# Reordering TensorE's program in a hedgehog-attention plus SwiGLU kernel: filler matmuls, moved query projections, merged evictions, spread gate/up groups

## Chip, cores, metric

One core of one Trainium2 chip. The metric is the device time of one execution in microseconds (us). Profiles show a "span" some 2 us shorter than that time (277.9 where the execution took 279.78). Ratios in this text are the mean time of one kernel's fast runs over the mean of the other's fast runs of the same rounds, so not quite the ratio of the medians quoted beside them.

## The reference, cut to what matters

```python
xn = layernorm(x)                                # x: (1, 2048, 640)
# A: linear attention, 32 heads of 20
q, k, v = split(xn @ wqkv)
phi(t)  = concat(softmax(t @ w_phi), softmax(-(t @ w_phi)))   # 40 features per head
kv = sum_s phi(k) v ; z = sum_s phi(k)
o  = phi(q) @ kv / (phi(q) @ z + 1e-6)
A  = o @ wo
# B: SwiGLU, 640 -> 1536 -> 640
B  = (silu(xn @ w1) * (xn @ w3)) @ w2
out = x + A + B
```

## The kernel before

All work is described as operations with an engine, a modelled duration and dependencies; a small planner puts them in an order per engine. In the profile of this kernel, TensorE (PE) ran nothing else during the 1.40 us that the KV product at 135.53 us waited for phi_k. The names used below, for 16 tiles of 128 tokens in 4 chunks `c` of 512:

- `T(t)`, `V(t)`, `K(t)`: transpose of a tile, value and key projections. `KV(t)`: ten small matmuls that add a tile's phi(k) and v into two PSUM tiles `kva` and `kvb`. `kv_evac`: their masked copy to SBUF (`kvr`).
- `Q(c, g)`: query projection of a chunk, group `g` of 5 (five 128x512 matmuls), followed on ScalarE (ACT) by two exponentials `eq`.
- `RT(t)`: twelve matmuls `eq x kvr`, whose results ACT copies to `rt`; half go to PSUM tiles named `rtbank`, of which there are only two.
- `ATT(pair)`, `OT(pair)`: division on VectorE (DVE), then a store (`od`) and a transposing DMA (`oT`).
- `GU(c, fi)`: one gate/up group, ten 128x512 matmuls, then ACT (`th`, `up`), DVE (`gs`), GpSimd (POOL, `hT`).
- `O(t)`: an output tile, two halves of twelve `w2` and five `wo` matmuls.
- `fill(us)`: puts in as many GU groups as the PE time that is owed.

```python
    def warm():                       # ten 128x512 matmuls at the start
    ...
    def fill(us):
        nonlocal gi, owed
        owed += us
        while owed > 1.1 and gi < limit:
            GU(*gus[gi], modes(gi)); gi += 1
            owed -= 2.16
    ...                               # (cut: the loop over K, V, KV; at its end gi has met limit)
    KV(NST - 2)
    fill(2.2)
    KV(NST - 1)
    kv_evac()                         # 20 evictions of 84 columns
    wo_dma = ...
    for g in range(NQ):
        Q(0, g)

    def attend(pair, us):
        RT(2 * pair); fill(us); RT(2 * pair + 1); ATT(pair); OT(pair); fill(us)

    residual(0)
    limit = 3 * KF
    attend(0, 2.2)
    attend(1, 2.2)
    for i in range(NST // 2):
        nxt = i + 2
        if i % 2 == 0 and nxt // 2 < NSC:
            residual(nxt // 2)
            for g in range(NQ):
                Q(nxt // 2, g)
        if nxt < NST // 2:
            attend(nxt, 2.2)
        if i == 5:
            fill(100)
        O(2 * i)
        O(2 * i + 1)
        if i == 1:
            limit = len(gus)
```

The softmax here doesn't subtract the row's maximum and nothing guards it: scores larger than these inputs give would overflow.

## Time and profile before

| | before |
|---|---|
| time, 4 runs known at the time of the prediction | 285.73 us (285.39 to 285.8) |
| time, 16 runs by the end of the comparison | 285.91 us (285.25 to 288.1) |
| span of the profiled run | 283.3 us |
| PE busy | 271.2 us, 96% |
| last matmul group of PE starts | 278.91 us |

PE is nearly always busy, so what can be won is its holes. The prediction below shows the lines and how a hole is measured from them.

### The profile page before, as it was taken

How to read it: one execution, taken by the hardware profiler on the slowest of the kernel's cores; microseconds unless marked ns; L12 is line 12 of the kernel's file. 1: busy time of each engine (PE TensorE's matmuls, PEld its weight loads, DVE VectorE, ACT ScalarE, POOL GpSimd, SP SyncE). 2: the span in 40 equal slices, each digit the busy share in tenths (PEclk: the TensorE clock that was granted, in tenths of full speed). 3: DMA queues.
4: the chain of work that ended last, by engine and by line, in shares of the span. 5: the costliest groups of instructions: out<-in, count | busy, mean ns of one | idle time of the engine just before them, and what ended most of it. 6: DMA issues, size and time to landing. Idle time of an engine off the chain costs nothing.

```text
span 283.3 us, 4874 instructions
## 1 busy us (share of the span) xinstructions
PE 271.2 (96%) x1863; PEld 163.6 (58%) x1886; DVE 172.0 (61%) x295; ACT 146.1 (52%) x320; POOL 94.6 (33%) x124
## 2 busy tenths in 40 slices
PE   7899999999998999998899999999999999999994
PEld 2545555556565556565445567644457675777773
DVE  4783699979767655668626986414458280657221
ACT  2668766666675767665769904284460508340000
POOL 8734657747546555554032000003331100000000
PEclk9999999999999999999999999999999999999999
DMA  8999995027000700003000344340001316042301
GB/s 220 312 299 249 282 288 189 0 74 175 33 0 0 187 1 2 0 0 119 0 0 2 91 139 98 108 126 0 0 2 44 98 57 175 2 139 70 94 23 46
DMA packets 44614, 26.54 MB, mean 94 GB/s; under 512 B 26288, under 2 KB 44592, under 8 KB 44592
## 3 DMA queue, kind: packets, MB, share of 16 engines
q1 hardware_dynamic: 43936, 26.22, 33.3%
q8 instruction: 14, 0.23, 0.3%
q10 hardware_dynamic: 656, 0.03, 0.2%
q14 instruction: 8, 0.07, 0.1%
HBM read 12.81 MB, written 7.21 MB: 71 GB/s over the span
## 4 chain that ended last, share of the span: by engine, by line
PE 76%; issue 7%; DVE 6%; ACT 5%; DMA 3%; POOL 1%; SPq 1%; DVEq 0%; ACTq 0%; POOLq 0%
PE bank L548 35%; PE bank L790 14%; PE bank L399 12%; PE bank L794 6%; PE bank L636 4%; ACT eq L651 2%; DMA xg<-in_A_x_dram 2%; ACT rt L690 1%; DVE ks L447 1%; PE rtbank L682 1%; PE bank L505 1%; DVE om L731 1%; ACT ek L438 1%; DMA oT<-od 1%; DVE phik L464 1%
## 5 line engine op out<-in xcount | busy, mean ns | idle before, releaser
L548 PE MATMUL bank<-xnT,w 128*128 128x512 bf16 x461 | 108.3, 379 | 1.8 <-DVE gs L569 0.8
L591 POOL TENSOR_TENSOR hT<-gs,up 128x512 bf16<-128x512 bf16 x44 | 50.8, 1155 | 118.5 <-ACT up L586 81.2
L548 PEld LDWEIGHTS <-w 128*128 128x128 bf16 x480 | 46.7, 98 | 51.7 <-issue 1.0
L790 PE MATMUL bank<-w,hT 128*128 128x320 bf16 x384 | 59.1, 299 | 0.0
L569 DVE SCALAR_TENSOR_TENSOR gs<-th,bank 128x512 bf16<-128x512 bf16 x48 | 32.4, 677 | 36.2 <-ACT th L564 36.2
L790 PEld LDWEIGHTS <-hT 128*128 128x128 bf16 x384 | 37.2, 98 | 13.8
L564 ACT ACTIVATE th<-bank 128x512 bf16<-128x512 f32 x48 | 28.9, 602 | 23.0 <-PE bank L548 22.7
L399 PEld LDWEIGHTS <-xnT 128*128 128x128 bf16 x320 | 30.3, 98 | 14.9 <-DVE xnT L385 1.1
L586 ACT ACTIVATE up<-bank 128x512 bf16<-128x512 f32 x44 | 26.3, 597 | 23.4 <-PE bank L548 23.4
L447 DVE TENSOR_REDUCE ks<-ek 128x64 f32<-128x1280 bf16 x16 | 23.6, 1476 | 16.6 <-ACT ek L438 16.5
L651 ACT ACTIVATE eq<-bank 128x512 bf16<-128x512 f32 x40 | 21.4, 649 | 21.6 <-PE bank L636 21.6
L464 POOL TENSOR_TENSOR phik<-ek,kr 128x640 bf16<-128x640 bf16 x16 | 29.1, 1820 | 6.7 <-PE bank L399 3.0
L799 DVE TENSOR_TENSOR res<-bank,xr 128x320 bf16<-128x320 f32 x32 | 15.4, 484 | 23.0 <-PE bank L794 23.0
L794 PE MATMUL bank<-wo,oT 128*128 128x320 bf16 x160 | 26.9, 299 | 0.6 <-DMA oT<-od 0.6
L690 ACT CAST rt<-bank 128x352 bf16<-128x352 f32 x32 | 13.9, 522 | 24.5 <-issue 15.1
L399 PE MATMUL bank<-wv,xnT 128*128 128x320 bf16 x160 | 24.4, 299 | 1.6 <-DVE xnT L385 0.8
L438 ACT ACTIVATE ek<-bank 128x320 bf16<-128x320 f32 x64 | 23.1, 439 | 3.7 <-PE bank L399 3.5
L399 PE MATMUL bank<-wkphi,xnT 128*128 128x320 bf16 x160 | 24.3, 299 | 0.0
L464 DVE TENSOR_TENSOR phik<-ek,kr 128x640 bf16<-128x640 bf16 x16 | 22.1, 1381 | 1.8 <-DVE kr L456 0.5
L636 PE MATMUL bank<-xnT,wqphi 128*128 128x512 bf16 x96 | 22.5, 379 | 0.2
L794 PEld LDWEIGHTS <-oT 128*128 128x128 bf16 x160 | 15.6, 98 | 7.0 <-DMA oT<-od 1.0
L682 PEld LDWEIGHTS <-eq 128*128 128x128 bf16 x192 | 12.8, 98 | 7.1 <-ACT eq L651 2.3
(62 smaller groups left out, 216.4 us busy)
## 6 DMA issues: line engine op xcount, KB each, us to landing
w<-in_B_w_dram SPq DMA_DIRECT2D x8, 480.0 KB, 7.0
xr<-in_A_x_dram SPq DMA_DIRECT2D x4, 640.0 KB, 4.7
od<-om SPq DMA_DIRECT2D x8, 320.0 KB, 2.3
out_dram<-res SPq DMA_DIRECT2D x16, 160.0 KB, 2.0
xg<-in_A_x_dram SPq DMA_DIRECT2D x12, 160.0 KB, 3.8
xnd<-xn SPq DMA_DIRECT2D x3, 640.0 KB, 3.2
w<-in_B_w_dram SPq DMA_DIRECT2D x1, 1920.0 KB, 10.0
wv<-in_A_wqkv_dram SPq DMA_DIRECT2D x2, 400.0 KB, 4.2
```

Of the source, the lines that this page charges most:

```text
L399: nc.tensor.matmul(o["ps"][:], xnT[:, c, t * P : (t + 1) * P], w[:, c, 320 * half : 320 * half + 320], start=(c == 0), stop=(c == KD - 1),)
L447: nc.vector.reduce_sum(out=box["s"][:].rearrange("p a h -> p (a h)"), in_=box["ek"][:].rearrange("p a (h d) -> p (a h) d", d=Dh), axis=AX.X,)
L464: phik_ins[t] = eng.tensor_mul(out=phik_b[t][:, :, sgn, :], in0=box["ek"][:, sgn, :].rearrange("p (h d) -> p h d", d=Dh), in1=box["r"][:, ...
L548: nc.tensor.matmul(o["ps"][:], w[:, k, fi * P : (fi + 1) * P], xs[:, k, :], start=(k == 0), stop=(k == KD - 1))
L564: nc.scalar.activation(out=box["th"][:], in_=og["ps"][:], func=AF.Tanh, scale=0.5)
L569: nc.vector.scalar_tensor_tensor(out=box["gs"][:], in0=box["th"][:], scalar=1.0, in1=og["ps"][:], op0=ALU.add, op1=ALU.mult)
L586: nc.scalar.activation(out=box["up"][:], in_=ou["ps"][:], func=AF.Copy, scale=0.5)
L591: lambda: nc.gpsimd.tensor_mul(out=hT[c][:, fi, :], in0=box["gs"][:], in1=box["up"][:]),
L636: nc.tensor.matmul(o["ps"][:], wqphi[:, k, g * P : (g + 1) * P], xnT[:, k, c * 512 : (c + 1) * 512], start=(k == 0), stop=(k == KD - 1),)
L651: nc.scalar.activation(out=eqt[c, sgn][:, g, 0:512], in_=o["ps"][:], func=AF.Exp, scale=1.0 - 2.0 * sgn)
L790: nc.tensor.matmul(o["ps"][:], hT[c][:, fi, ti * P : (ti + 1) * P], w2[:, fi, cols], start=(fi == 0), stop=False)
L794: nc.tensor.matmul(o["ps"][:], oT[c][:, k, ti * P : (ti + 1) * P], wo_of[0][:, k, cols], start=False, stop=(k == KD - 1))
```

## The change

The intent is to close PE's holes: keep it busy at the start, place the query projections where PE waits for the last keys, evict in fewer instructions, stop gate/up groups from coming in bursts, keep RT groups apart, and do both `w2` halves of the first output tile before its `oT` is needed. Core of the diff:

```diff
+        load_x(xg[1], 0, 4, 1)
         load_gu(0)
-        load_x(xg[1], 0, 4, 1)
...
+    def idle(n):                       # n matmuls 128x256 on a tile of zeros
...
     T(0, "DVE")
+    keep_busy(9)                       # nine of them as one operation of the planner
...
     T(1, "ACT")
+    keep_busy(6)
...
-                    for k in range(g, e):
-                        nc.vector.tensor_mul(out=dst[:, k, ...], in0=v[:, k, ...], in1=m[:, k, ...])
+                    nc.vector.tensor_mul(out=dst[:, g:e, ...], in0=v[:, g:e, ...], in1=m[:, g:e, ...])
...                                     # O(t) is split in first (w2) and second (wo):
+            [(first, 0), (first, 1), (second, 0), (second, 1)] if t == 0
+            else [(first, 0), (second, 0), (first, 1), (second, 1)]
...                                     # in fill():
+        if gi == limit:
+            owed = 0.0
...
+    fill(2.2)
+    Q(0, 0)
     KV(NST - 2)
-    fill(2.2)
+    for g in range(1, 4):
+        Q(0, g)
     KV(NST - 1)
     kv_evac()
     wo_dma = ...
-    for g in range(NQ):
-        Q(0, g)
+    Q(0, 4)
+    fill(2.2); RT(0)                   # RT 1 to 3 likewise, each behind a fill
...                                     # the loop, for i, with nxt = i + 2:
+            fill(2.2); RT(2 * nxt); fill(2.2)
         O(2 * i)
+            RT(2 * nxt + 1); ATT(nxt); OT(nxt)
+        if nxt % 2 == 1 and nxt // 2 + 1 < NSC:
+            for g in range(NQ): Q(nxt // 2 + 1, g)
         O(2 * i + 1)
```

More of the change, by code (lines that the diff above doesn't have):

```diff
@@ L183 @@
     ident = consts.tile([P, P], bf, name="ident")
+    zero = consts.tile([P, 256], bf, name="zero")
     eps = consts.tile([P, 1], f32, name="eps")
@@ L210, in warm, with fn @@
             nc.tensor.matmul(ps[:], xnT[:, 0, 0:P], xnT[:, 0, 0:512])
+    def idle(n):
+        def fn():
+            ps = bank([P, 256], f32)
+            for i in range(n):
+                nc.tensor.matmul(ps[:], zero[:, 0:P], zero[:])
+        return fn
     WARM = 10
@@ L215, in constants @@
         make_identity(nc, ident[:])
+        nc.gpsimd.memset(zero[:], 0.0)
         nc.gpsimd.memset(eps[:], EPS)
@@ L368, in bank, with keep_busy @@
         return ringp.tile(shape, dt, name="bank", tag="bank")
+    def keep_busy(n):
+        u = plan.op("PE", pe_us(n, 256), idle(n), takes="bank")
+        u["frees"].append(u)
+        u["open"] += 1
     def T(t, evac):
@@ L610, in fn @@
                 def fn(g=g, e=e):
-                    for k in range(g, e):
-                        nc.vector.tensor_mul(
-                            out=dst[:, k, offs[g] : offs[g] + 4, 0 : HC - 1],
-                            in0=v[:, k, :, :],
-                            in1=m[:, k, :, None].to_broadcast([64, 4, HC - 1]),
-                        )
-                kvr_of.append(plan.op("DVE", 0.2 * (e - g), fn, deps=[KV_of[NST - 1]]))
+                    nc.vector.tensor_mul(
+                        out=dst[:, g:e, offs[g] : offs[g] + 4, 0 : HC - 1],
+                        in0=v[:, g:e, :, :],
+                        in1=m[:, g:e, :, None].to_broadcast([64, e - g, 4, HC - 1]),
+                    )
+                kvr_of.append(plan.op("DVE", dve_us(84 * (e - g)), fn, deps=[KV_of[NST - 1]]))
                 g = e
@@ L772, in OT, with O @@
         )
-    def O(t):
+    def O(t, between=None):
         c, ti = divmod(t, 4)
@@ L782, in O, with first, fn @@
         rb = plan.alloc("half", al)
-        for half in range(2):
-            cols = slice(320 * half, 320 * half + 320)
-            o = {}
-            def fn(o=o, cols=cols):
+        hs = [dict(cols=slice(320 * h, 320 * h + 320), half=h) for h in range(2)]
+        def first(o):
+            def fn():
                 o["ps"] = bank([P, 320], f32)
@@ L790, in fn, with second, ev @@
                     nc.tensor.matmul(
-                        o["ps"][:], hT[c][:, fi, ti * P : (ti + 1) * P], w2[:, fi, cols], start=(fi == 0), stop=False
+                        o["ps"][:], hT[c][:, fi, ti * P : (ti + 1) * P], w2[:, fi, o["cols"]], start=(fi == 0), stop=False
                     )
+            o["u"] = plan.op("PE", pe_us(KF, 320), fn, deps=GU_of[c], takes="bank", frees=[hT_a[c]])
+        def second(o):
+            def fn():
                 for k in range(KD):
-                    nc.tensor.matmul(o["ps"][:], oT[c][:, k, ti * P : (ti + 1) * P], wo_of[0][:, k, cols], start=False, stop=(k == KD - 1))
-            u = plan.op("PE", pe_us(KF + KD, 320), fn, deps=GU_of[c] + [dep, wo_dma], takes="bank", frees=[oT_a[c], hT_a[c]])
-            def ev(o=o, cols=cols, half=half):
-                nc.vector.tensor_tensor(out=box["res"][:, cols], in0=o["ps"][:], in1=xr[c][:, ti, cols], op=ALU.add)
-                if half == 1:
-                    nc.sync.dma_start(out=out2[t * P : (t + 1) * P, :], in_=box["res"][:])
-            plan.op("DVE", dve_us(320), ev, deps=[u, xr_of[c], rb], frees=[u, xr_a[c]] + [rb] * half)
+                    nc.tensor.matmul(o["ps"][:], oT[c][:, k, ti * P : (ti + 1) * P], wo_of[0][:, k, o["cols"]], start=False, stop=(k == KD - 1))
+            o["v"] = plan.op("PE", pe_us(KD, 320), fn, deps=[o["u"], dep, wo_dma], frees=[oT_a[c]])
+            def ev():
+                nc.vector.tensor_tensor(out=box["res"][:, o["cols"]], in0=o["ps"][:], in1=xr[c][:, ti, o["cols"]], op=ALU.add)
+                if o["half"] == 1:
+                    nc.sync.dma_start(out=out2[t * P : (t + 1) * P, :], in_=box["res"][:])
+            plan.op("DVE", dve_us(320), ev, deps=[o["v"], xr_of[c], rb], frees=[o["u"], xr_a[c]] + [rb] * o["half"])
+        for step in (
+            [(first, 0), (first, 1), (second, 0), (second, 1)] if t == 0
+            else [(first, 0), (second, 0), (first, 1), (second, 1)]
+        ):
+            step[0](hs[step[1]])
     xr_of = {}
@@ L890 @@
     wo_dma = plan.op("SP", 0.5, load_wo, deps=[KV_of[NST - 1]], lat=3.5)
-    for g in range(NQ):
-        Q(0, g)
-    def attend(pair, us):
-        RT(2 * pair)
-        fill(us)
-        RT(2 * pair + 1)
-        ATT(pair)
-        OT(pair)
-        fill(us)
+    Q(0, 4)
     residual(0)
     limit = 3 * KF
-    attend(0, 2.2)
-    attend(1, 2.2)
+    fill(2.2)
+    RT(0)
+    fill(2.2)
+    RT(1)
+    ATT(0)
+    OT(0)
+    fill(2.2)
+    RT(2)
+    fill(2.2)
+    RT(3)
+    ATT(1)
+    OT(1)
+    for g in range(NQ):
+        Q(1, g)
     for i in range(NST // 2):
         nxt = i + 2
-        if i % 2 == 0 and nxt // 2 < NSC:
-            residual(nxt // 2)
-            for g in range(NQ):
-                Q(nxt // 2, g)
         if nxt < NST // 2:
-            attend(nxt, 2.2)
+            if nxt % 2 == 0:
+                residual(nxt // 2)
+            fill(2.2)
+            RT(2 * nxt)
+            fill(2.2)
         if i == 5:
@@ L916 @@
         O(2 * i)
+        if nxt < NST // 2:
+            RT(2 * nxt + 1)
+            ATT(nxt)
+            OT(nxt)
+        if nxt % 2 == 1 and nxt // 2 + 1 < NSC:
+            for g in range(NQ):
+                Q(nxt // 2 + 1, g)
         O(2 * i + 1)
```

## The prediction

> **What bounds the kernel now.** I read the page first (busy shares), then busy time by stretch, then the list of waits, then TensorE's (PE's) timeline around the waits found, and last the order of instructions of both programs on each engine.
>
> ```profile
> PE 271.2 (96%) x1863; PEld 163.6 (58%) x1886; DVE 172.0 (61%) x295; ACT 146.1 (52%) x320; POOL 94.6 (33%) x124
> ```
>
> PE is busy 96% of 283.3 us. Busy includes the modelled tail of each matmul, so short gaps hide in it. The stretches show where idle time lies (columns: stretch, length, busy time of PE, weight loads, DVE, ACT, POOL, each with a count):
>
> ```profile
> 5.00:15.00 10.00, 7.87 (x62) 5.14 (x61) 7.93 (x25) 5.85 (x13) 7.58 (x36) 1.00 1.14 311
> 126.00:136.00 10.00, 8.29 (x85) 5.82 (x85) 6.55 (x6) 5.65 (x15) 4.32 (x3) 1.00 0.26 84
> 150.00:164.00 14.00, 12.85 (x105) 7.77 (x105) 11.82 (x24) 12.50 (x31) 1.15 (x1) 1.00 0.22 60
> 190.00:235.00 45.00, 44.74 (x282) 26.45 (x286) 25.09 (x42) 15.85 (x32) 9.22 (x8) 1.00 0.11 34
> 255.00:283.30 28.30, 24.75 (x183) 17.61 (x180) 9.27 (x17) 0.00 (x0) 0.00 (x0) 1.00 0.19 58
> ```
>
> The reader is to see that 190 to 235 us runs without gaps, so this program can feed PE, and that holes stand at the start, at 126 to 136, at 150 to 164, and at the very end (the last eviction and store). The waits of PE itself (total, times, longest):
>
> ```profile
> PE kva L481 <- DVE phik L464: 1.4, 1, 1.4
> PE bank L794 <- DMA oT<-od: 0.6, 1, 0.6
> PE rtbank L682 <- ACT rt L690: 0.5, 3, 0.2
> PE kva L481 <- POOL phik L464: 0.3, 1, 0.3
> PE bank L682 <- ACT eq L651: 0.2, 1, 0.2
> ```
>
> and the places on PE's timeline (start, length, line, operation, count, wait):
>
> ```profile
> 131.48 0.20 PE L481 MATMUL kva<-vaug,phik 128*128 128x84 bf16 x1
> ...
> 135.53 0.20 PE L481 MATMUL kva<-vaug,phik 128*128 128x84 bf16 x1 [1.40 <-DVE phik L464]
> ...
> 140.01 0.44 PE L682 MATMUL bank<-kvr,eq 128*128 128x154 bf16 x5
> ...
> 149.63 0.51 PE L682 MATMUL bank<-kvr,eq 128*128 128x154 bf16 x6
> ...
> 157.68 0.37 PE L682 MATMUL bank<-kvr,eq 128*128 128x154 bf16 x4
> ...
> 163.73 0.85 PE L794 MATMUL bank<-wo,oT 128*128 128x320 bf16 x5 [0.64 <-DMA oT<-od]
> ```
>
> The 1.40 us is the last KV product (line 481) waiting for the last phi_k; 163.73 is the first output tile waiting for its transposed attention output.
>
> [...] a group of ten 128x512 matmuls advances 2.16 us. [...] here the wait at 135.53 held up everything behind it. So what counts is the order on PE. [...] here the ten warm-up matmuls take 4.45 us (half rate) and the first projection at 7.05 runs at full rate; the largest wait of PE before 15 us is 1.24. [...] Below, 20 evictions of 84 elements take about 177 ns each [...].
>
> **Method.** I count PE's time in issue steps read from this timeline, not in busy time: 0.216 us per 128x512 matmul, 0.136 per 128x320 (17 in 2.31), 0.0573 in RT (24 in 1.375), 0.0385 in KV (10 in 0.385). Stretch minus work is time lost:
> - 131.86 (131.48 + 10 KV) to 140.01: 20 KV 0.77 + 25 Q matmuls 5.40 = 6.17 of 8.15; lost 1.98.
> - to 149.63: one RT 0.69 + 40 gate/up (GU) matmuls 8.64 = 9.33 of 9.62; lost 0.29.
> - to 157.68: three RT 2.06 + Q 5.40 = 7.46 of 8.05; lost 0.59 (three RT in a row wait for ACT to empty the two extra PSUM banks).
> - to 163.73: two RT 1.38 + 24 w2 matmuls 3.26 = 4.63 of 6.05; lost 1.42 (exponentials of Q, then the oT transfer).
> - to PE's last issue, about 279.6: 520 output matmuls 70.6 + ten RT 6.9 + two Q 10.8 + twelve GU 25.9 = 114.2 of 115.9; lost 1.65, at 170 to 172, 182 to 188, 239 to 243 and 250 to 253, where RT follows RT or Q.
>
> In all 1.98 + 0.29 + 0.59 + 1.42 + 1.65 = 5.93 us. That is all that a perfect order after 131.86 could win.
>
> **The change part by part.** The programs' orders on PE differ only by the two fillers until 131.86.
>
> *Start.* Nine zero matmuls after transpose 0 and six after transpose 1, 128x256: about 0.107 each at full rate, 0.96 and 0.64 us. The holes there are 0.83 to 1.1 and 0.79 us, so they fit; at half rate nine take 1.9 and push projection 0 from 7.05 to about 8.0. Its end, 9.3 instead of 8.4, then passes transpose 1's start at 9.11: cost 0 to 0.3. No gain, since the clock is already at full rate. Moving the second x block (640 KB) ahead of the first gate/up weights (2 x 480 KB) keeps the same bytes ahead of both: x lands near 10.3 instead of 12.5 and the weights near 12.5, estimated from x landing 7.7 us after issue at 4.84 and 300 GB/s. The weights are first used at 15.04 and DVE turns to that x only after 12.9. Worth 0.
>
> *KV end.* Q groups 0 to 3 now stand around KV 14 and 15. KV 15 comes 131.86 + 1.08 + 0.39 + 3.24 = 136.57, after phi_k (135.5); KV 14 at 132.94, after its own (132.3). Both waits vanish.
>
> *kvr.* Twenty DVE evictions, 3.55 us, become eight of the same elements. [...]
>
> ```profile
> 136.07 0.85 DVE L612 TENSOR_TENSOR kvr<-kva,mask 64x84 bf16<-64x84 f32 x5 [0.69 <-PE kvb L481]
> ```
>
> They begin at about 137.1 and end at 139.6. Ahead of RT 0 PE has Q group 4 and one GU: 136.96 + 1.08 + 2.16 = 140.2. The merge is needed for this order but by itself off the path.
>
> *Spreading.* Setting owed to zero removes the bursts of four and ten GUs; one GU goes between RTs. Per step PE needs 2.85 us; ACT two evictions at 0.6 and four rt copies at 0.343 (twelve in 4.11), 2.57. ACT keeps up, the PSUM waits go. Q 1 then RT 4 remains adjacent: ten exponentials take 5.17 to 5.4 us against PE's 5.4, so the last ends about 1.2 to 1.4 us after Q while RT's other ten matmuls and three of w2 fill 1.0. I keep a loss of 0.4. Q 2 and Q 3 now have a whole output tile behind them.
>
> *First output.* Both w2 halves go first. Attention of pair 0 ends on DVE near 152.0 (rt copies done 145.3, then 5.3 us of its own work and two gs); plus 2.3 for od and 3.7 for oT gives 158.0. PE arrives after RT 1 to 4, three more GUs, Q 1 and 24 w2 matmuls, at about 159.3. No wait. At the other end, RT 15 ends near 251, its oT lands near 265, and tile 14 needs it after 266: no wait, 1.7 us to spare.
>
> **Sum.** 5.93 won; 0.4 left at RT 4; 0.4 kept for small new waits and the fillers: 5.1 us. 285.73 - 5.1 = 280.6.
>
> **Rivals.**
> 1. *Perfect packing*: PE loses nothing after 131.86: 285.73 - 5.93 = 279.8. For: 190 to 235 us is nearly free of gaps. Against: ACT is busy 12.50 of 14 us in 150 to 164, and it is still behind Q 1.
> 2. *A new wait replaces the old*: DVE or ACT, in order, are held by an attention step or a th whose source is late, and the spread GUs feel it each time. For: each GU needs ACT, then DVE, and DVE now has gs inside attention. Twelve to sixteen places at 0.15 would give back 2: 282.5.
> 3. *The start gets worse*: fillers at half rate, or weights late. Loses 0.3 to 1; with the main gain 281 to 281.6.
> 4. *Holes were hidden anyway*: that would need another bound, but PE is the last engine throughout; the idle DVE and ACT time after 163 speaks against it. Then 285.
>
> **Range and chances.** Faster by over 2% means below 280.0, a gain of 5.7 out of 5.93: nearly perfect packing. I give it 0.22. Between 280.0 and 282.5, small remains or rival 2, is the bulk; slower by 2% would need a stall of 10 us, 0.01. Range 279.4 to 282.5.
>
> **What would show it.** Right: no wait of a kva/kvb matmul on phi_k; no wait of the first wo matmul on oT; eight kvr evictions of about 2.5 us in all; RT waits on rt copies gone; RT 4's first matmul near 155 and the first wo matmul near 159 us; fillers ahead of the first projections, with GU still starting near 15.0. Wrong: PE idle by DVE's gs or ACT's th between 140 and 260, a wait on w1 near 15 us, a later first projection, or a wait for oT at tile 14.

## The result and the profile after

| | before | after |
|---|---|---|
| median time | 285.91 us (285.25 to 288.1, 16 runs) | 279.84 us (279.5 to 280.43, 11 runs) |
| ratio | | 0.9782, 95% interval 0.9761 to 0.9803 |
| span of the profiled run | 283.3 | 277.9 |
| start of PE's last matmul group | 278.91 | 273.35 |
| start of the first `wo` group | 163.73 | 159.11 |

The kernel is 2.2% faster; the interval straddles the 2% line, so whether the gain passes 2% is unclear. Busy time of the changed kernel in stretches like those of the prediction (length, then PE, weight loads, DVE, ACT, POOL, then granted clock, DMA share and GB/s):

```profile
5.00:15.00 10.00, 9.59 (x77) 6.66 (x76) 7.89 (x26) 5.78 (x13) 7.83 (x37) 1.00 1.16 288
126.00:136.00 10.00, 9.95 (x86) 6.55 (x86) 6.56 (x6) 7.06 (x18) 4.31 (x3) 1.00 0.27 84
150.00:164.00 14.00, 14.00 (x103) 8.76 (x101) 11.04 (x20) 9.06 (x21) 1.61 (x1) 1.00 0.37 92
190.00:235.00 45.00, 44.79 (x326) 29.22 (x329) 24.39 (x44) 17.81 (x40) 3.46 (x3) 1.00 0.22 64
```

PE went from 8.29 to 9.95 of 10 us in the second stretch and from 12.85 to 14.00 of 14 in the third, while ACT fell there from 12.50 to 9.06. In the first stretch the new busy time is the fillers, which compute nothing. All waits of PE that remain in the changed kernel (total, times, longest):

```profile
PE bank L211 <- DVE xnT L208: 1.2, 1, 1.2
PE bank L563 <- DVE gs L584: 0.8, 1, 0.8
PE bank L392 <- DVE xn L337: 0.3, 1, 0.3
```

The waits on phi_k, oT, rt copies and eq are gone from this list. The three that it has are not new: the kernel before has the same kinds (xnT 1.2, gs 0.8, xn 0.5), and two further waits for xnT of 0.8 each. The prediction's list, which shows five of the ten, left them out. PE's timeline of the changed kernel, at the places that answer to those of before (L496 is the KV product, L696 RT, L803 `w2`, L812 `wo`):

```profile
136.59 0.20 PE L496 MATMUL kva<-vaug,phik 128*128 128x84 bf16 x1
...
140.21 0.51 PE L696 MATMUL bank<-kvr,eq 128*128 128x154 bf16 x6
...
154.84 0.44 PE L696 MATMUL bank<-kvr,eq 128*128 128x154 bf16 x5
...
155.69 0.24 PE L696 MATMUL bank<-kvr,eq 128*128 128x154 bf16 x1
...
156.18 0.24 PE L696 MATMUL rtbank<-kvr,eq 128*128 128x154 bf16 x1
...
159.11 1.52 PE L812 MATMUL bank<-wo,oT 128*128 128x320 bf16 x10
...
273.35 0.84 PE L812 MATMUL bank<-wo,oT 128*128 128x320 bf16 x5
```

The last KV product stands at 136.59 without a wait (predicted 136.57), RT 0 at 140.21 (140.2), RT 4 at 154.84 ("near 155"), the first `wo` matmul at 159.11 ("about 159.3"). From the end of KV 13 to PE's last issue (last group's start plus 5 x 0.136) before took 279.59 - 131.86 = 147.73 us and after 274.03 - 131.90 = 142.13, for work of 141.8: of 5.93 us lost there, 5.6 are won and 0.3 remain, most of it around the two single matmuls at 155.69 and 156.18, gaps of some 0.15 us each, too short for the list of waits; ACT ends the last exponentials of Q 1 near 156.1.

### The profile page after: what moved, and what is told of

It is laid out like the page before. It is cut to its first block, busy times and chain, and to the rows that moved or that the text cites. A ratio compares the mean times of both kernels' runs of the same rounds, so it can differ in the third digit from the quotient of the medians.

```text
span 277.9 us, 4892 instructions
## 1 busy us (share of the span) xinstructions
PE 270.5 (97%) x1877; PEld 165.6 (60%) x1901; DVE 173.1 (62%) x283; ACT 146.5 (53%) x320; POOL 95.4 (34%) x125
## 4 chain that ended last, share of the span: by engine, by line
PE 91%; DVE 2%; DMA 2%; issue 1%; POOL 1%; ACT 1%; SPq 1%; POOLq 0%
PE bank L563 35%; PE bank L803 19%; PE bank L414 14%; PE bank L812 8%; PE bank L650 8%; PE bank L696 2%; PE rtbank L696 2%; DMA xg<-in_A_x_dram 2%; PE bank L520 1%; PE kva L496 1%; PE kvb L496 1%; POOL phik L479 1%; DVE gs L584 0%; ACT ek L453 0%; POOL rstd L308 0%
## 5 line engine op out<-in xcount | busy, mean ns | idle before, releaser
L606 POOL TENSOR_TENSOR hT<-gs,up 128x512 bf16<-128x512 bf16 x44 | 51.2, 1165 | 140.2 <-ACT up L601 91.7
L803 PE MATMUL bank<-w,hT 128*128 128x320 bf16 x384 | 57.5, 299 | 0.0
L803 PEld LDWEIGHTS <-hT 128*128 128x128 bf16 x384 | 37.4, 98 | 15.0
L704 ACT CAST rt<-bank 128x352 bf16<-128x352 f32 x32 | 12.9, 458 | 29.7 <-PE bank L696 25.9
L812 PE MATMUL bank<-wo,oT 128*128 128x320 bf16 x160 | 26.8, 299 | 0.0
L812 PEld LDWEIGHTS <-oT 128*128 128x128 bf16 x160 | 15.7, 98 | 6.1
L650 PEld LDWEIGHTS <-wqphi 128*128 128x128 bf16 x100 | 9.5, 98 | 10.4
```

Source lines behind the costliest of these rows:

```text
L606: lambda: nc.gpsimd.tensor_mul(out=hT[c][:, fi, :], in0=box["gs"][:], in1=box["up"][:]),
L650: nc.tensor.matmul(o["ps"][:], wqphi[:, k, g * P : (g + 1) * P], xnT[:, k, c * 512 : (c + 1) * 512], start=(k == 0), stop=(k == KD - 1),)
L803: nc.tensor.matmul(o["ps"][:], hT[c][:, fi, ti * P : (ti + 1) * P], w2[:, fi, o["cols"]], start=(fi == 0), stop=False)
L812: nc.tensor.matmul(o["ps"][:], oT[c][:, k, ti * P : (ti + 1) * P], wo_of[0][:, k, o["cols"]], start=False, stop=(k == KD - 1))
```

## The experiments

Twelve runs were made, one of them the changed kernel again, each with a correct result and timed in rounds against the kernel before on the same chip. "Part undone" kernels are the changed kernel less one part; "part alone" kernels are the kernel before plus one. The differences in us below are between medians, 279.84 for the changed kernel and, for parts alone, the median of before of the same rounds. The parts undone ran in other rounds than those that gave 279.84; the changed kernel, repeated beside c_all, gave 279.81.

### Parts undone

**Fillers out (a_nofill).** Edit:

```diff
-    keep_busy(9)
-    keep_busy(6)
```

> The changed kernel without its fifteen zero matmuls at the start. Theory (the prediction's): [...] they are worth 0 in a typical execution: 279.8 +- 0.3, gate/up starting at 15.0 to 15.1 us. Rival: they keep the PE clock up; then projections 0 and 1 run at half rate without them in the profile, or some executions come out 1.5 to 2.5 us above the rest, as three of the sixteen executions of the kernel before did (287.6 to 288.1), while none of eleven of the changed kernel did.

Measured 280.68 us median (279.87 to 283.77, 6 runs), ratio to before 0.9829 (interval 0.9777 to 0.9882). Two of six executions were at 282.85 and 283.77, the fastest at 279.87. That is the rival's picture: not the fastest execution but the spread. The theory of "worth 0" fails for a typical execution; with six runs its size is not well fixed, so the fillers were also run alone, below. The rival's other sign, a half rate in the profile, did not show: in the profiled execution (280.37) the first projection takes 1.53 us for ten matmuls. Gate/up begins there at 15.59 us, not at 15.0 to 15.1 as expected; after_again, with fillers, begins at 15.55, so the missing fillers need not be the reason.

**Twenty evictions (a_kvr20).** Edit: the loop over `k` back in place of the one `tensor_mul`.

> The changed kernel with the twenty small kvr evictions of the kernel before. Theory: eight merged ones took 2.74 us in the changed kernel's profile, twenty take 3.55; they would end near 140.7 us where RT 0 stands at 140.2, so the wait is 0.3 to 0.5 us: 280.0 to 280.4, and PE shows a wait of RT 0 on kvr. Rival: the merge is worth its 0.8 us of DVE time in full, because DVE falls behind for the rest of the attention: 280.6 or more. Second rival: nothing, 279.8.

Measured 279.88 us, ratio 0.9784: no difference, the second rival. The evictions did end at 140.87 instead of 139.87, but PE shows no wait. The scheduler had put two gate/up matmuls into RT 0; PE's timeline of this kernel:

```profile
140.38 0.51 PE L697 MATMUL bank<-kvr,eq 128*128 128x154 bf16 x6
140.72 0.34 PE L697 MATMUL rtbank<-kvr,eq 128*128 128x154 bf16 x3
140.89 0.60 PE L563 MATMUL bank<-xnT,w 128*128 128x512 bf16 x2
141.33 0.34 PE L697 MATMUL rtbank<-kvr,eq 128*128 128x88 bf16 x3
```

The first six matmuls of RT 0 read only the half of `kvr` that is written first; they start at 140.38, when the other half is still being written.

**First output tile unsplit (a_onosplit).** Edit: `if t == 0` made false, so that tile 0 goes half by half.

> The changed kernel with tile 0 of the output in the old order (w2 and wo of one half, then the other). Theory: the first wo matmul then stands at about 157.5 us and oT lands at 154.7 + 3.6 = 158.3, so PE waits about 0.9 us: 280.5 to 280.9, with a wait of wo on the oT transfer. Rival: the spreading of the other work brings oT early enough and the split is worth nothing: 279.8.

Measured 280.92 us (280.44 to 281.51), ratio 0.9816: 1.1 us slower, slightly more than expected (in the profiles the last group starts 1.21 later, of which 0.34 was there before KV 14, so 0.87 is the tile's), and the wait is back in the list of PE's waits:

```profile
PE bank L812 <- DMA oT<-od: 0.7, 1, 0.7
```

**Bursts back (a_burst).** Edit:

```diff
-        if gi == limit:
-            owed = 0.0
```

> The changed kernel without setting the debt to zero at the limit, so that gate/up groups come in bursts again (four ahead of RT 0, ten in the second half) in the new loop. Theory: RT 0 to 3 stand next to each other again and wait for ACT to free the two extra PSUM banks (0.6 us lost in the kernel before) and ACT is later for Q 1 (another 0.3 to 0.8); in the second half the new loop keeps RT apart by output tiles, so nothing is lost there: 280.5 to 281.3. Rival: the spreading is the main source of the gain and this gives back 2 us or more: 282 or more.

Measured 281.86 us (281.64 to 282.26), ratio 0.9849: 2.0 us slower, between theory and rival. Place and mechanism are the theory's, the size is not. By PE's timeline the whole loss lies ahead of the first output:

```profile
138.23 8.80 PE L563 MATMUL bank<-xnT,w 128*128 128x512 bf16 x39
...
148.83 0.33 PE L696 MATMUL rtbank<-kvr,eq 128*128 128x154 bf16 x3 [0.29 <-ACT rt L704]
...
161.05 0.57 PE L803 MATMUL bank<-w,hT 128*128 128x320 bf16 x3
162.40 1.53 PE L812 MATMUL bank<-wo,oT 128*128 128x320 bf16 x10 [0.78 <-DMA oT<-od]
```

Four gate/up groups in a row (138.23) push all RT back; pair 0's attention then starts later and PE waits for oT although tile 0 is split. In the changed kernel RT 5 and all `w2` of the second output tile come after the first `wo` group. Here RT 5 (0.69) and three of these `w2` matmuls (0.41, at 161.05) stand before it, and this execution entered the stage 0.17 later: 162.40 - 0.69 - 0.41 - 0.17 - 159.11 = 2.0 us, which is the whole loss. The expectation had left out the oT wait. The second half loses nothing, as expected: the last group starts at 275.55, 2.2 after the changed kernel's, or 2.0 without the 0.17.

**Old order at the end of the keys (a_oldkv).** Edit: the `KV`, `Q(0, g)` block of before put back, gate/up group and all else as changed.

> The changed kernel with the old order at the end of the key phase: KV 14, KV 15, then all of Q 0. Theory: the waits of KV 14 and KV 15 on phi_k return, 1.7 us of idle time shown and 1.98 by issue steps: 281.5 to 281.9. Rival: the work behind (spread gate/up, first output tile) has slack that takes up part of it, since PE is later than the DVE and DMA chains there: 280.3 to 281.2.

Measured 281.99 us (281.56 to 282.25), ratio 0.9867: 2.15 us slower, the theory's 1.98 nearly. In the profiles the last group starts 2.23 later, of which 0.25 was there before KV 13, so 1.98 remain. The waits return:

```profile
PE kva L496 <- DVE phik L479: 1.4, 1, 1.4
...
PE kva L496 <- POOL phik L479: 0.3, 1, 0.3
```

**Old loop over pairs (a_oldloop).** Edit: `attend` and the loop of before put back after `OT(1)`, all else as changed.

> The changed kernel with the old loop over pairs (Q and both RT of a pair first, then both output tiles), all else changed. Theory: RT stands next to RT or Q again for the later chunks: most of the 1.65 us lost after 163.7 in the kernel before returns, and 0.2 to 0.5 around the first output tile: 281.4 to 282. Rival: the zeroed debt alone spreads enough work between them, so that only the pairs without gate/up between them lose: 280.3 to 281.

Measured 280.99 us (280.92 to 281.46), ratio 0.9836: 1.15 us slower. That is at the upper end of the rival: with the debt zeroed, gate/up groups stand between most RTs in the old loop too, and only the places without one lose (RT 6 and 7 at 166 to 168 us, and after each Q).

### Parts alone

**Debt zeroed alone (b_reset).** Edit: the two lines of `fill` added to the kernel before.

> The kernel before with only the debt set to zero at the limit. Theory: gains the 0.59 us of RT 1 to 3 and part of the 0.29 and of the exponentials' wait, keeps both phi_k waits; in the second half the ten-group burst is spread over pairs that were tight: in all 1.2 to 2 us: 283.9 to 284.7. Rival: spreading is the change that matters: 282.5 or less. Second rival: nothing, since what PE gains between RTs it waits for at oT: 285.5.

Measured 283.71 us (283.01 to 284.33, 8 runs) against 285.41, ratio 0.9923: 1.7 us by medians and 2.2 by the ratio of means. The theory's 1.2 to 2.

**Query projections moved alone (b_kv).** Edit: the new `KV`/`Q` block in the kernel before, without the merged evictions and without a gate/up group ahead of RT 0.

> The kernel before with only Q 0 moved around KV 14 and KV 15, the kvr evictions still twenty and no gate/up group between Q and RT 0. Theory: the phi_k waits vanish (1.7 us), but RT 0 now stands at about 138.0 us while the evictions end near 140.7, so PE waits there instead, for up to 2.6 us less what gate/up matmuls can be slipped in: no gain, 285.5 to 286.6. Rival: the move is worth its 1.7 to 2 us alone: 283.9 to 284.2.

Measured 283.64 us (283.04 to 287.25, 22 runs) against 285.41, ratio 0.9941 (0.9922 to 0.9961): 1.8 us by medians, the rival. The expected wait on the evictions is hardly there, as PE's timeline shows:

```profile
137.19 1.24 PE L636 MATMUL bank<-xnT,wqphi 128*128 128x512 bf16 x5
138.53 0.50 PE L682 MATMUL bank<-kvr,eq 128*128 128x154 bf16 x4
138.87 0.38 PE L548 MATMUL bank<-xnT,w 128*128 128x512 bf16 x1
139.08 0.51 PE L682 MATMUL bank<-kvr,eq 128*128 128x154 bf16 x2
139.43 1.24 PE L548 MATMUL bank<-xnT,w 128*128 128x512 bf16 x5
140.51 0.23 PE L682 MATMUL rtbank<-kvr,eq 128*128 128x154 bf16 x1
```

RT 0 begins at 138.53, while its own `kvr` tile is being finished, and the second half of RT 0 is spread among eight gate/up matmuls that fill the time until the other tile is done at 140.92. I had let all of RT 0 wait for all twenty evictions, and had looked at the program, not at the built order, for what stands between.

**The two parts priced at zero (b_zero).** Edit: merged evictions and the x block loaded first, in the kernel before.

> The kernel before with the two parts that the prediction priced at zero by themselves: the merged kvr evictions and the second x block loaded ahead of the first gate/up weights. Theory: PE's order is unchanged, RT 0 is held by Q and not by kvr, and both loads land before use: same as the kernel before within 0.1%. Rival: the earlier x moves the second LayerNorm and the later loads, or the merge lets RT 0 start earlier: 0.5 us or more faster.

Measured 285.39 us (284.79 to 288.19, 22 runs) against 285.91, ratio 0.9991 (0.9974 to 1.0008): zero, as expected. The medians differ by 0.5 us all the same, so a difference of that size between medians says little where some executions are slow. Its profile happened to catch something else, at the start of PE's timeline:

```profile
5.64 0.71 PE L377 MATMUL bank<-ident,xn 128*128 128x128 bf16 x5
7.04 2.85 PE L399 MATMUL bank<-wv,xnT 128*128 128x320 bf16 x10 [0.68 <-DVE xnT L385]
9.68 0.74 PE L377 MATMUL bank<-ident,xn 128*128 128x128 bf16 x5
...
15.89 0.38 PE L548 MATMUL bank<-xnT,w 128*128 128x512 bf16 x1
```

Ten 128x320 matmuls took 2.85 us; the same ten take 1.53 in the profile of the kernel before, and the first gate/up group starts at 15.89 instead of 15.04. PE ran at half rate until past 10 us in this execution. The granted clock of this very stretch, in the column after the counts, still says 1.00:

```profile
5.00:15.00 10.00, 8.54 (x56) 5.24 (x55) 7.19 (x23) 5.09 (x11) 7.72 (x36) 1.00 1.16 302
```

**Fillers alone (b_fill).** Edit: the tile of zeros, `idle`, `keep_busy` and its two calls in the kernel before.

> The kernel before with only the fifteen zero matmuls added. The prediction said worth 0 because the profile of before showed a full clock from 7 us on; since then the kernel with the two priced-at-zero parts showed projection 0 at half rate in its profile (2.85 us for ten matmuls, gate/up starting at 15.89 instead of 15.04), and executions 1.5 to 3 us above the rest were seen only in kernels without the fillers. Theory now: the clock at the start varies from execution to execution and the fillers settle it: the fastest executions stay at 285.0 to 285.4, all lie within 1.3 us of each other, and the mean is 0.4 to 0.7 us below that of before: ratio 0.9975 to 0.9985. Rival: the fillers do nothing and the slow executions have another cause: some executions at 287 or above, ratio 1.000.

Measured 285.39 us (285.04 to 286.21, 22 runs) against 286.0 (285.19 to 288.16, 27 runs) in the same rounds, ratio 0.9973 (0.9958 to 0.9987): 0.7 us by means, 0.6 by medians. b_zero's medians differ as much, so what shows the effect is the interval and the tail: the fastest executions are the same, the slow ones are gone. This agrees with all the other runs: of the kernels with fillers, none has executions more than 1.2 us apart, and those without them have ranges of 1.3 us (b_reset, 8 runs) to 4.2 (b_kv, 22 runs). The profiled execution of b_fill had its hole elsewhere (the first projection waited until 8.22 for DVE) but ran at full rate from 5.5 us on:

```profile
5.80 1.15 PE L217 MATMUL bank<-zero 128*128 128x256 bf16 x9
8.22 1.53 PE L414 MATMUL bank<-wv,xnT 128*128 128x320 bf16 x10 [1.28 <-DVE xnT L400]
```

That the half-rate start of b_zero is what the slow executions have in common is an inference: gate/up started 0.85 us later there than before, but it starts anywhere from 14.90 to 16.10 in the other profiles without a half-rate projection, while the slowest executions are 2.5 to 3 us out, and none of those was profiled.

The record has more on them than I used: every run lists its mean granted clock. Of 94 executions of the kernel before beside these experiments, 13 took over 287 us, and 11 of the 13 have a mean granted clock of 0.993 or less, seven of them 0.986. In all 74 executions of kernels with fillers it is 0.997 or more. So a lowered clock goes with most of the tail, and the fillers remove both. At which point of the execution it was low is not shown, and three slow executions (287.15 of before, 287.25 of b_kv, 283.77 of a_nofill) read 1.000; their cause stays open.

### A version that beats both

**Four more repairs (c_all)** at places where the changed kernel still loses time. Edits, in short:

```diff
+        fill(1.95)                       # LN(2) and LN(3) come one fill later,
         if t == 5 or t == 9:
             LN((t + 3) // 4)
-        fill(1.95)
...                                     # and stay behind the last gs on DVE:
-    ds = [ln_apply(4 * c + i, [a]) for i in range(4)]
+    late = gs_ops[-1] if c >= 2 else (None, None)
+    ds = [ln_apply(4 * c + i, [a, late[0]], late[1]) for i in range(4)]
...                                     # RT 4 between w2 and wo of tile 0:
-            RT(2 * nxt)
+            if i > 0:
+                RT(2 * nxt)
...
-        O(2 * i)
+        O(2 * i, (lambda: RT(4)) if i == 0 else None)
...                                     # second half of wv after x tile 2, not after tile 1:
-            if t < 2:
+            if t in (0, 2):
...                                     # last tile stored in two halves:
+                if t == NST - 1:
+                    nc.sync.dma_start(out=out2[..., o["cols"]], in_=box["res"][:, o["cols"]])
```

> The changed kernel with four more repairs at places where its profile still shows PE idle: the LayerNorm applications of chunks 2 and 3 put behind a gate/up product on DVE (PE waits 0.77 us at 89.4 for a gs that stands behind an application waiting for POOL), RT 4 put between the w2 and the wo matmuls of tile 0 (0.4 us lost at 155.5), the third x tile loaded ahead of the second half of wv, and the last tile stored in two halves. Theory: 0.9 + 0.4 + 0.2 + 0.1: 278.2 to 278.6. Rival: the LayerNorm made later brings xnT late for K 8 or K 12, or the waits move on as PE gets there earlier: 279.3 to 280.

> The changed kernel again, on the same chip and in the same rounds as the kernel with the four more repairs: 279.8 +- 0.3, ratio to the kernel before 0.978.

Measured 278.34 us (278.26 to 279.19, 5 runs), ratio to before 0.9741 (0.9709 to 0.9773); the changed kernel, in the same rounds, 279.81 (279.67 to 280.21), ratio 0.9786. So 1.5 us more, faster than both. All waits of PE left in it:

```profile
PE bank L211 <- DVE xnT L208: 1.2, 1, 1.2
PE bank L396 <- DVE xn L338: 0.7, 2, 0.4
PE bank L568 <- DVE gs L589: 0.2, 1, 0.2
```

The gate/up group that waited until 89.36 now starts at 88.23, where 0.2 of the difference is an earlier start of the program (gate/up from 14.90 instead of 15.11); the single RT matmuls waiting for exponentials are gone, with 24 `w2` matmuls behind Q 1. I did not run the four repairs one by one.

## Why the prediction was right, point by point

- *What bounds the kernel; what can be won.* Right. PE's order was the bound, 5.93 us were to be had after 131.86, and 5.6 were won. Both key-end (a_oldkv, b_kv) and spreading (a_burst, b_reset) are worth about 2 us each, the unsplit tile and the old loop about 1.1 each. Single undoings sum to 6.4 with the key end, bursts, tile and loop alone, more than the 5.6, plausibly because they share waits: part of the burst's loss is the same oT wait that the split tile removes (0.78 us in a_burst, 0.69 in a_onosplit).
- *KV end.* Right to 0.02 us in place, and 2.15 by medians, 1.98 by profiles, against 1.98 us in size.
- *kvr.* The zero was right, the reason was half wrong. "The merge is needed for this order" failed: undone, it costs 0.04 us (a_kvr20), and the moved projections pay without it (b_kv). RT 0's two halves need different `kvr` tiles, and gate/up matmuls slip in between. The eight evictions took 2.74 us (137.13 to 139.87), not the 2.5 of the prediction, which was the author's estimate. Twenty took 3.55 in the profile of before (3.57 in a_kvr20), so twelve instructions fewer over the same elements saved 0.81 us: by these two profiles, as an estimate, 0.07 us each.
- *Spreading.* The mechanism was right. Left at RT 4: 0.4 predicted; 0.3 is all that is lost in the whole stretch after 131.90.
- *First output.* Right: no wait, 159.11 against about 159.3; unsplit it costs 1.1 us.
- *Start.* Here a step failed: "No gain, since the clock is already at full rate" was read from one profile, and the rate at the start differs between executions: the ten matmuls of the first projection took 1.53 us in the profile of before and 2.85 in that of b_zero. What sets that rate, no run here shows. The fillers at full rate took what was predicted, 0.107 us each (half the 0.216 of a 128x512 matmul): nine took 1.15 us and six 0.82 in b_fill, 0.11 for each of the three more; in the changed kernel's profile the nine took 1.46. Alone the fillers are worth 0.27%, 0.7 us of the mean, and most of the spread. Moving the x block, run together with the merge, was worth zero, as said. One of the listed signs of being wrong did show: the first projection starts later, at 7.37 against 7.05. But it starts at 7.37 without the fillers too (a_nofill), so they need not be the cause, and gate/up starts at 15.11, near the 15.0 named.
- *The 0.4 us kept for new waits and fillers* did not come. Rival 2 did not show: between 140 and 260 us the list has no wait of PE on DVE or ACT, and the two gaps of 0.15 us at RT 4 are all that is seen of one. The median came out 0.76 us below the predicted 280.6. The stretch after KV 13 explains 0.5 of it (5.6 won against 5.1); the rest is within what the fillers' gain can be, and also within the noise of medians. Rival 1, perfect packing at 279.8, came nearest. The 0.22 given to more than 2% looks low, since the fillers were counted as cost only; whether the gain passes 2% stays unclear.

## What to carry to other kernels

When one engine is busy 96% of the time, add up its work in issue steps and subtract it from the clock: that gives the whole sum that a reordering can win, and each hole then has an address. PE ran nothing during its wait of 1.40 us for phi_k, and moving ready work in front of the wait filled that hole (PE busy 8.29, then 9.95 of 10 us at 126 to 136); what decides is the built order, where a scheduler may already have slipped other work between. One profile shows one execution: a spread of the times that a profile does not explain, here 285.25 to 288.1, is itself something to test. The mean granted clock of the runs that were not profiled is a first thing to look at.

## What the traces showed of TensorE

- Groups of ten 128x512 matmuls advance 2.16 us (80.66 to 82.82 in the profile of before, 80.70 to 82.86 in that of the changed kernel), 216 ns each, weight loads included.
- The rate at the start varies between executions. In the profile of before the five transposes at 5.51 us took 0.71 us, so PE was slow until after 6, and the projection at 7.05 took 1.53; in b_zero the projection at 7.04 took 2.85 and the transposes at 9.68 still 0.74, so PE was slow until past 10. There the wait ahead of the slow projection was 0.68 us, and the longest wait before it 1.24. Fifteen small zero matmuls in such gaps took the spread from 3.0 us (before, 27 runs) to 1.2 (b_fill, 22 runs), and the mean down by 0.27%. That the gaps kept the clock down in b_zero is not shown by itself.
- In b_zero, five 128x128 transposes took 0.71 us at 5.64 and 0.74 at 9.68, on either side of the slow projection, and 0.44 from 11.89 us on.
- In b_zero the granted clock of 5 to 15 us reads 1.00, although ten 128x320 matmuls took 2.85 us there, and 1.53 in the profile of before; only the durations showed it.
